# Fewer and smaller weight conversions in the last twelve ticks of attention

## The chip, the cores and the metric

The kernel runs on one NeuronCore of a Trainium2 chip. The metric is the time on the device in microseconds (us). Three runs of the kernel before took 709.95, 710.32 and 710.77 us; their median, 710.32 us, is the time before. The core's engines are TensorE (PE, with its weight loads as PEld), VectorE (DVE), ScalarE (ACT), GpSimd (POOL) and SyncE (SP), which only issues DMAs here. Each engine works through its own instructions in the order in which they are written, and waits on semaphores for the others.

## The reference, cut to what matters

Three stages, each feeding the next, all in float32:

- attention, for 2 batches of 8 heads, 768 positions, head size 64: scores `q k^T / 8`, masked where two hash buckets (signs of a projection to 6 values) differ, softmax over the row, times `v`;
- a dense layer on the 1536 rows of 512 values that come out: `h = x @ w_in` (512 to 2048), `g = s * max(h, 0)^2 + b`, `x2 = g @ w_out` (2048 to 512);
- a layer of 8 experts (512 to 1024 to 512) with one expert for each row, scaled by a softmax gate and a sigmoid gate.

## The kernel before, in words

**Attention** is a loop of 96 ticks (`tick`). A tick handles 128 query rows of one head against 768 keys. A pair of heads takes 12 ticks, and three ticks with one head's half of the queries form a trio. In tick t TensorE computes the scores `sp` (L264, L265); VectorE takes the row maximum `nm` (L267) and adds a constant to the sum of the tick before (`rd`, L272), then takes its reciprocal (L316); ScalarE computes the exponentials `pe` with their row sum (L323); GpSimd scales `pe` of the tick before by the reciprocal (L317). Three ticks later TensorE turns the probabilities around in two groups of three blocks (`tp`, L284) and each group is copied out of PSUM into `pt` (L312). At the end of each trio TensorE multiplies three of those blocks for both heads with `v` (`xp`, L333). `sp` has two buffers, so the scores of tick t+2 wait for the exponentials of tick t; `tp` has two buffers too, so the transposes of a tick wait for the copies of the tick before.

Within a tick, ScalarE's queue holds the copies of `tp` first and the exponentials behind them. VectorE's queue holds `nm`, `rd`, in some ticks the second copy of `tp`, the reciprocal, the low halves of attention's output (`xl`, L319), and last a piece of a weight conversion where there is one. The second copy is VectorE's in ticks whose number modulo 12 is 3, 4 or 6 (`VCOPY`), and in the drain (ticks 96 and later). In ticks 0 to 83 the queues also hold the preparation of the next pair of heads; ticks 84 to 95 belong to the last pair and have none. The ticks named below are 84 to 95.

**Dense-layer weights** come from HBM as 16 blocks of 1 MB, each holding a column block of `w_in` and a row block of `w_out` (k = 0 and 1). `stage(j)` loads block j as two tiles `stg` (512 KB each; five buffers; blocks 10 and 13 use a tile `tmp` instead). `conv(j)` turns each into a high part and a low part in the format that the matmuls want: per k, VectorE does L358, L360 and L364 into `cvm`, ScalarE rounds the result to the high part (L365), and VectorE subtracts to get the low part (L367). `conv` is a generator; what stands between two `yield`s is issued in one go. In the kernel before it has three pieces: both L358 and both L360; both L364, both L365 and the first L367; the second L367. In ticks 84 to 95 one piece follows each tick: blocks 0, 1 and 2 take ticks 84 to 92, and ticks 93 to 95 have none.

**The dense layer** (`moe1`) runs 48 steps, 16 for each third of the rows. Step s issues two ticks of attention's drain while there are any, then the 12 matmuls of `mm1` with block s mod 16 (L380), the nonlinearity of step s-1 (`elem` on ScalarE, `elem2` on VectorE, whose L402 writes `gl`), and the 12 matmuls of `mm2` for step s-2 (L418 to L420). Steps 0 to 12 stage block s+5 and convert block s+3 in one go. In VectorE's queue the conversion stands ahead of `gl` of step s-1; in ScalarE's, behind `elem`. A step is 24 matmuls.

Of the kernel before, what the change touches and what calls it, by code (L numbers as in the profile page):

```python
# [14 lines left out]
ALU = mybir.AluOpType  # L15
# [26 lines left out]
VCOPY = (3, 4, 6)  # L42
# [3 lines left out]
class Kernel:  # L46
# [190 lines left out]
    def tick(self, t):  # L237
        nc = self.nc
        NQ = 96
# [20 lines left out]
        if t < NQ:  # L260
            sp = self.ps2.tile([128, 2, 512], F32, tag="big", name="sp")
            for m in range(2):
                k = slice(m * HS, (m + 1) * HS)
# [11 lines left out]
        if 0 <= a < NQ:  # L275
            pe3, _ = st["pe"].pop(a)
# [10 lines left out]
        if t >= 15 and (t - 15) % 6 == 0:  # L287
# [11 lines left out]
            while lo < t0 + HS:  # L299
                g, c = divmod(lo, GW)  # L300
# [8 lines left out]
                lo = hi  # L309
        run("act")  # L310
        for j, c in enumerate(tps):
            (nc.vector.tensor_copy if j and (t % 12 in VCOPY or t >= NQ) else nc.scalar.copy)(*c)  # L312
        run("pool")
        run("dve")
        if 1 <= t < NQ + 1:
# [32 lines left out]
            nc.sync.dma_start(out=t, in_=self.ins["wio"][j, k])  # L348
            self.stg[j, k] = t

    def conv(self, j):
        nc = self.nc
        pool = self.wpool(j)
        self.w[j] = pool.tile([128, 2, 2, 512], F32R, tag="w", name="w")
        t = [self.stg.pop((j, k)) for k in range(2)]
        m = [self.cv_p.tile([128, 512], I32, name="cvm", bufs=4) for k in range(2)]
        for k in range(2):
            nc.vector.tensor_scalar(m[k], t[k][:, :, 1], 3, 0x3FFFFFFF, ALU.logical_shift_left, ALU.bitwise_and)  # L358
        for k in range(2):
            nc.vector.scalar_tensor_tensor(m[k], t[k][:, :, 1], -0x40000000, m[k], ALU.bitwise_and, ALU.bitwise_or)  # L360
        yield
        w = self.w[j]
        for k in range(2):
            nc.vector.scalar_tensor_tensor(m[k], t[k][:, :, 0], 29, m[k], ALU.logical_shift_right, ALU.bitwise_or)  # L364
            nc.scalar.copy(w[:, k, 0, :], m[k].bitcast(F32))  # L365
        for k in range(2):
            nc.vector.tensor_tensor(w[:, k, 1, :], m[k].bitcast(F32), w[:, k, 0, :].bitcast(F32), ALU.subtract)  # L367
            yield
# [566 lines left out]
    def moe1(self, ticks):  # L935
        self.h, self.g, self.y = {}, {}, {}
        gates = iter(())
        seq = self.sequence(0, NSTAT, {2})
        sp = iter(())
        self.ring, self.nring, self.nht, self.lq, self.regs, self.routed = {}, 0, 0, [], {}, False  # L940
        self.xg, self.xt, self.ht, self.hs, self.yps, self.hts = {}, {}, {}, {}, {}, []
        ns = 16 * NG
        for s in range(ns + 2):
            g, j = divmod(s, 16)
            for _ in range(2):
                next(ticks, None)
            c = s + 3
            cv = iter(())
            if c < 16:
                if c + 2 < 16:  # L950
                    self.stage(c + 2)
                cv = self.conv(c)
            if s < ns:
                self.mm1(s)
            if s > ns - 15:
                next(gates, None)
            if 1 <= s < ns + 1:
                self.elem(s - 1)
            for _ in cv:
                pass  # L960
            if 1 <= s < ns + 1:
                self.elem2(s - 1)
            if s >= 2:
                self.mm2(s - 2, gates if s > ns - 15 else iter(()))
                if (s - 2) % 16 == 15:
                    for _ in gates:
                        pass
                    gates = self.gate((s - 2) // 16)
                    if s == ns - 15:
                        self.x_es.close()  # L970
                        self.m2_p = self.m2_open()
                        gates = chain(gates, self.route_early())
            next(gates, None)
            for k in range(AHEAD):
                if s == ns + (-4, -3, -1, 0)[k]:
                    sp = chain(sp, self.split(seq[k], True))
            for _ in range(3):
                next(sp, None)
            if s == ns - 2:
                self.tx(0)  # L980
        for _ in sp:
            pass
        self.moe2(seq, chain(gates, self.route()), NSTAT)
# [28 lines left out]
    def build(self):  # L1012
        tc = self.tc
        with ExitStack() as es:
            ent = es.enter_context
            sb = lambda n, b, side="left": tc.tile_pool(name=n, bufs=b, side=side, reuse_waits="tile")
            ps = lambda n, b: tc.tile_pool(name=n, bufs=b, space=PSUM, reuse_waits="tile")
            dr = ent(tc.tile_pool(name="dr", bufs=1, space=DRAM))
            self.x2d = dr.tile([TOK, XW], F32, name="x2d")
            ent(tc.manual_schedule())  # L1020
            cst = ent(sb("cst", 1))
            self.stg_p = ent(sb("stg", 5))
            self.sg_p = ent(sb("sg", 1))
            self.ps1 = ent(ps("ps1", 1))
            ps_es = ExitStack()
            self.ps2 = ps_es.enter_context(ps("ps2", 2))
            self.x_es = ExitStack()
            self.x3_p = ent(sb("x3", 1, "right"))
            self.x_p = self.x_es.enter_context(sb("x", 1, "right"))
            self.m2_open = lambda: ent(sb("m2", 1, "right"))  # L1030
            self.stg, self.w = {}, {}
            self.consts(cst)
            e1 = ExitStack()
            r1 = lambda n, b: e1.enter_context(sb(n, b, "right"))
            self.v_p, self.xs_p, self.sm_p = r1("v", 3), r1("xs", 1), r1("sm", 6)
            self.p_p, self.pt_p = r1("pp", 5), r1("ptp", 4)
            e2 = ExitStack()
            r2 = lambda n, b: e2.enter_context(sb(n, b, "right"))
            self.qk_p, self.bit_p = r2("qk", 2), r2("bit", 2)
            self.cv_p = ent(sb("cv", 1))  # L1040
            with sb("d", 2, "right") as self.d_p:
                self.attention()
            self.w_p = [ent(sb("wa", 3))]

            def convs():
                for c in range(3):
                    for _ in self.conv(c):
                        yield
                    self.stage(c + 2)
            cv = convs()  # L1050
            for t in range(84, 96):
                self.tick(t)
                next(cv, None)
            for _ in cv:
                pass
            e2.close()
            ps_es.close()
            self.ps4 = ent(ps("ps4", 4))
            self.w_p.append(ent(sb("wb", 5)))
            self.g_p = ent(sb("g", 2))  # L1060

            def drain():
                for t in range(96, 107):
                    self.tick(t)
                    if t == 106:
                        e1.close()
                        self.w_p.append(ent(sb("wc", 8)))
                    yield
            self.moe1(drain())
            if "x2" in self.debug:  # L1070
                self.nc.sync.dma_start(out=self.debug["x2"], in_=self.x2d)
            self.T = self.nc.values_load(self.ev[0:1, 40:41], min_val=0, max_val=NMAX - 2)  # L1072
            self.extra(NSTAT)
# [67 lines left out]
```

## Time and profile before

| | |
|---|---|
| median of three runs | 710.32 us |
| profiled execution | 710.86 us |
| its span, first to last instruction | 709.1 us |
| PE busy | 679.8 us (96%) |
| DVE busy | 486.0 us (69%) |
| ACT busy | 421.9 us (60%) |
| POOL busy | 166.9 us (24%) |
| mean granted TensorE clock | 0.993 of full |

All positions in time are microseconds from the start of the profiled execution's span. Busy time of an engine is the time that its instructions cover. A line of a timeline gives start, duration, engine, source line, operation, tiles and shape; "x2" merges two neighbours, whose second starts before the first's end is recorded, so a pair's duration is less than twice that of one. In square brackets stands how long the engine was idle ahead of it, and who ended that.

### The profile page before, as it was taken

Reading aid. Unit: us, or ns where it says so; the run is one execution under the profiler, and the core shown is the slowest. Engines: PE = TensorE matmul, PEld = TensorE weight load, DVE = VectorE, ACT = ScalarE, POOL = GpSimd, SP = SyncE. Lnnn points to the kernel's source line nnn. Section 1 sums busy time; section 2 is a strip of 40 time slices with the busy share of each in tenths; the row PEclk is TensorE's granted clock in tenths of the full one; section 3 lists DMA queues with packets and bytes.
Section 4 is the critical chain, followed back from the end, with each engine's and each line's share of the span. In section 5 each row is a group of like instructions: output and inputs, shape, how many; then the busy total and the mean of one; then the engine's idle time right before and its main releaser. Section 6 shows DMA issues by size and latency. Waiting matters only on the chain. (4 is left out here: it accounts for less than half of the span.)

```text
span 709.1 us, 10423 instructions
## 1 busy us (share of the span) xinstructions
PE 679.8 (96%) x3696; PEld 512.4 (72%) x3696; DVE 486.0 (69%) x945; ACT 421.9 (60%) x756; POOL 166.9 (24%) x182
## 2 busy tenths in 40 slices
PE   6799999999997899999999999999999899999995
PEld 3566666666765567888877888788888688888863
DVE  4977778868779888993333432463357998998980
ACT  3778778878785756665212222222344688888870
POOL 4655555655554410000000000001000121212111
PEclk9999999999999999999999999999999999999999
DMA  9943261450601336520000020028301262101482
GB/s 205 242 93 95 62 157 37 120 140 19 215 1 61 119 119 238 196 72 1 0 1 1 0 61 0 1 61 357 147 1 48 58 223 90 59 31 56 151 298 110
DMA packets 17577, 69.89 MB, mean 99 GB/s; under 512 B 2990, under 2 KB 3886, under 8 KB 14064
## 3 DMA queue, kind: packets, MB, share of 16 engines
q1 hardware_dynamic: 15472, 62.61, 28.5%
q0 software_dynamic: 2048, 6.56, 2.7%
q8 instruction: 31, 0.51, 0.3%
q14 instruction: 26, 0.21, 0.1%
HBM read 100.61 MB, written 6.43 MB: 151 GB/s over the span
## 5 line engine op out<-in xcount | busy, mean ns | idle before, releaser
L380 PE MATMUL h<-xh,w 128*128 128x512 f32 x384 | 129.9, 399 | 0.0
L773 DVE TENSOR_TENSOR ring<-raw,ring 128x1024 fp32r<-128x1024 f32 x96 | 113.6, 1222 | 11.5 <-ACT ring L771 10.4
L267 DVE TENSOR_REDUCE nm<-sp 128x1 f32<-128x768 f32 x96 | 91.3, 951 | 39.2 <-PE sp L265 38.4
L317 POOL TENSOR_SCALAR pe<-pe,rd 128x768 f32<-128x768 f32 x96 | 91.1, 949 | 108.0 <-DVE rd L316 47.4
L323 ACT ACTIVATE pe<-sp,nm 128x768 f32<-128x768 f32 x96 | 87.4, 910 | 20.5 <-DVE rd L272 16.0
L771 ACT CAST ring<-raw 128x1024 fp32r<-128x1024 f32 x96 | 96.4, 1054 | 1.6 <-DMA raw<-w 1.6
L312 ACT COPY pt<-tp 128x384 f32<-128x384 f32 x165 | 72.3, 487 | 28.1 <-PE tp L284 27.8
L284 PE MATMUL tp<-consts,pe 128*128 128x128 f32 x576 | 80.8, 277 | 5.8 <-POOL pe L317 2.3
L380 PEld LDWEIGHTS h<-xh,w 128*128 128x128 f32 x384 | 72.2, 188 | 18.4 <-issue 2.0
L264 PE MATMUL sp<-ka,qa 128*128 128x384 f32 x192 | 75.6, 394 | 7.1 <-ACT pe L323 5.1
L284 PEld LDWEIGHTS tp<-consts,pe 128*128 128x128 f32 x576 | 67.4, 142 | 15.6 <-POOL pe L317 8.6
L380 PE MATMUL h<-xl,w 128*128 128x512 f32 x192 | 76.0, 396 | 0.0
L396 ACT ACTIVATE gh<-r,sb 128x512 fp32r<-128x512 f32 x34 | 24.7, 725 | 85.5 <-PE y L420 42.8
L418 PE MATMUL y<-w,gh 128*128 128x512 f32 x192 | 75.5, 393 | 0.0
L419 PE MATMUL y<-w,gl 128*128 128x512 f32 x192 | 75.0, 391 | 0.0
L420 PE MATMUL y<-w,gh 128*128 128x512 f32 x192 | 74.9, 390 | 0.0
L333 PE MATMUL xp<-pt,v 128*64 128x384 f32 x384 | 70.2, 502 | 0.1
L265 PE MATMUL sp<-kb,qb 128*128 128x384 f32 x192 | 65.7, 342 | 0.0
L387 ACT ACTIVATE r<-h 128x512 f32<-128x512 f32 x48 | 28.8, 599 | 60.8 <-PE h L380 35.1
L264 PEld LDWEIGHTS sp<-ka,qa 128*128 128x128 f32 x192 | 36.9, 192 | 35.8 <-ACT pe L323 20.5
L404 DVE SCALAR_TENSOR_TENSOR gl<-r,sb,gh 128x512 fp32r<-128x512 f32 x34 | 25.6, 752 | 51.7 <-ACT gh L396 51.7
L625 POOL DMA_INDIRECT xg<-x2d,ix x2 | 2.3, 1145 | 213.9 <-DVE r L395 213.6
(234 smaller groups left out, 1156.7 us busy)
## 6 DMA issues: line engine op xcount, KB each, us to landing
raw<-w SPq DMA_DIRECT2D x56, 1024.0 KB
stg<-wio SPq DMA_DIRECT2D x28, 512.0 KB
d<-qk SPq DMA_DIRECT2D x14, 768.0 KB
dz<-qz SPq DMA_DIRECT2D x14, 384.0 KB
x2d<-x SPq DMA_DIRECT2D x12, 256.5 KB
v<-v SPq DMA_DIRECT2D x8, 384.0 KB
tmp<-wio SPq DMA_DIRECT2D x4, 512.0 KB
d<-qk SPq DMA_DIRECT2D x4, 384.0 KB
```

Of the source, the lines that this page charges most:

```text
L264: nc.tensor.matmul(sp[:, m, 0:HS], QA[h][:, q], KA[h][:, k], start=True, stop=False)
L267: nc.vector.tensor_reduce(nm, sp[:, :, 0:HS], AX.XY, ALU.max, negate=True)
L284: nc.tensor.transpose(tp[:, kt, :], pe3[:, (3 * j + kt) * 128:(3 * j + kt + 1) * 128], self.ident)
L312: (nc.vector.tensor_copy if j and (t % 12 in VCOPY or t >= NQ) else nc.scalar.copy)(*c)
L317: nc.gpsimd.tensor_scalar(pe, pe, rd, 1.0, ALU.mult, ALU.mult)
L323: nc.scalar.activation(pe.rearrange("p (n k) -> p n k", n=2), sp[:, :, 0:HS], AF.Exp, bias=nm, accum_out=den)
L380: nc.tensor.matmul(h, a, b, start=(n == 0), stop=(n == 11))
L418: nc.tensor.matmul(y, gh[:, c], w[:, 0], start=(j == 0), stop=False)
L419: nc.tensor.matmul(y, gl[:, c], w[:, 0], start=False, stop=False)
L420: nc.tensor.matmul(y, gh[:, c], w[:, 1], start=False, stop=(j == 15))
L771: nc.scalar.copy(t[:, 0], src)
L773: nc.vector.tensor_tensor(t[:, 1], src, t[:, 0].bitcast(F32), ALU.subtract)
```

## The change

Three edits. In ticks 84 to 95 the second copy of `tp` is ScalarE's as well, in all ticks (it was VectorE's in ticks 87, 88 and 90). The blocks converted in ticks 84 to 95 are 0 and 1 instead of 0, 1 and 2, with `conv` cut into six pieces: L358 and L360 of k = 0; the same of k = 1; L364 and L365 of k = 0; the same of k = 1; the two L367 apart. The twelve pieces fill the twelve ticks. In `moe1`, step s converts block s+2 instead of s+3 and stages block s+4 instead of s+5, in steps 0 to 13 instead of 0 to 12, and in one go as before.

```diff
-            (nc.vector.tensor_copy if j and (t % 12 in VCOPY or t >= NQ) else nc.scalar.copy)(*c)
+            (nc.vector.tensor_copy if j and (t % 12 in VCOPY and t < 84 or t >= NQ) else nc.scalar.copy)(*c)
...
-    def conv(self, j):
+    def conv(self, j, fine=False):
...
         for k in range(2):
             nc.vector.tensor_scalar(m[k], t[k][:, :, 1], 3, 0x3FFFFFFF, ALU.logical_shift_left, ALU.bitwise_and)
-        for k in range(2):
-            nc.vector.scalar_tensor_tensor(m[k], t[k][:, :, 1], -0x40000000, m[k], ALU.bitwise_and, ALU.bitwise_or)
-        yield
+            if fine:
+                nc.vector.scalar_tensor_tensor(m[k], t[k][:, :, 1], -0x40000000, m[k], ALU.bitwise_and, ALU.bitwise_or)
+                yield
+        if not fine:
+            for k in range(2):
+                nc.vector.scalar_tensor_tensor(m[k], t[k][:, :, 1], -0x40000000, m[k], ALU.bitwise_and, ALU.bitwise_or)
+            yield
         w = self.w[j]
         for k in range(2):
             nc.vector.scalar_tensor_tensor(m[k], t[k][:, :, 0], 29, m[k], ALU.logical_shift_right, ALU.bitwise_or)
             nc.scalar.copy(w[:, k, 0, :], m[k].bitcast(F32))
+            if fine:
+                yield
         for k in range(2):
             nc.vector.tensor_tensor(w[:, k, 1, :], m[k].bitcast(F32), w[:, k, 0, :].bitcast(F32), ALU.subtract)
             yield
...
-            c = s + 3
+            c = s + 2
...
-                for c in range(3):
-                    for _ in self.conv(c):
+                for c in range(2):
+                    for _ in self.conv(c, True):
                         yield
                     self.stage(c + 2)
```

VectorE's queue from the reciprocal of tick 84 on, in the kernel before (`nm` opens the next tick; `cvm` is the conversion's work tile, `stg` the staged weights):

```order
L316 RECIPROCAL rd<-rd 128x1
L358 TENSOR_SCALAR cvm<-stg 128x512 x2
L360 SCALAR_TENSOR_TENSOR cvm<-stg,cvm 128x512 x2
L267 TENSOR_REDUCE nm<-sp 128x1
L272 TENSOR_SCALAR rd<-den 128x1
L316 RECIPROCAL rd<-rd 128x1
L364 SCALAR_TENSOR_TENSOR cvm<-stg,cvm 128x512 x2
L367 TENSOR_TENSOR w<-cvm,w 128x512
```

The same queue from the same instruction on, with the change (L368 is the old L364):

```order
L316 RECIPROCAL rd<-rd 128x1
L358 TENSOR_SCALAR cvm<-stg 128x512
L360 SCALAR_TENSOR_TENSOR cvm<-stg,cvm 128x512
L267 TENSOR_REDUCE nm<-sp 128x1
L272 TENSOR_SCALAR rd<-den 128x1
L316 RECIPROCAL rd<-rd 128x1
L358 TENSOR_SCALAR cvm<-stg 128x512
L360 SCALAR_TENSOR_TENSOR cvm<-stg,cvm 128x512
L267 TENSOR_REDUCE nm<-sp 128x1
L272 TENSOR_SCALAR rd<-den 128x1
L316 RECIPROCAL rd<-rd 128x1
L368 SCALAR_TENSOR_TENSOR cvm<-stg,cvm 128x512
```

Between two `nm` there now stand two conversion instructions or one, where there were four or three, and the first piece now comes twice for a block, in two ticks running.

ScalarE's queue from the exponentials of tick 85 on, in the kernel before (`xs` is a copy of attention's output `xp` that falls into tick 87):

```order
L323 ACTIVATE pe,den<-sp,nm 128x768
L365 CAST w<-cvm 128x512 x2
L312 COPY pt<-tp 128x3x128 x2
L323 ACTIVATE pe,den<-sp,nm 128x768
L294 COPY xs<-xp 128x384
L312 COPY pt<-tp 128x3x128
L323 ACTIVATE pe,den<-sp,nm 128x768
L312 COPY pt<-tp 128x3x128
```

The same queue with the change, from the exponentials of tick 86 on (L369 is the old L365):

```order
L323 ACTIVATE pe,den<-sp,nm 128x768
L369 CAST w<-cvm 128x512
L294 COPY xs<-xp 128x384
L312 COPY pt<-tp 128x3x128 x2
L323 ACTIVATE pe,den<-sp,nm 128x768
L369 CAST w<-cvm 128x512
L312 COPY pt<-tp 128x3x128 x2
L323 ACTIVATE pe,den<-sp,nm 128x768
```

Ticks 86 and 87 now each end in one L369, and ticks 87 and 88 have both copies on ScalarE. TensorE's, SP's and GpSimd's instructions keep their order.

## Rows read from the trace of the kernel before

**Rows 1.** Windows: ticks 72 to 83, then the four trios of ticks 84 to 95.
```profile
core 0: us, PE busy (x) PEld busy (x) DVE busy (x) ACT busy (x) POOL busy (x), PEclk, DMA share, GB/s
184.65:212.90 28.25, 28.01 (x183) 19.48 (x181) 22.14 (x53) 22.73 (x52) 15.65 (x19) 1.00 0.19 71
212.90:219.69 6.79, 6.62 (x45) 4.80 (x43) 5.71 (x12) 3.59 (x9) 1.98 (x3) 1.00 0.00 0
219.69:232.48 12.79, 9.10 (x45) 5.15 (x43) 12.46 (x26) 7.81 (x18) 4.95 (x6) 0.87 0.33 119
232.48:239.56 7.08, 6.92 (x44) 4.72 (x43) 6.73 (x15) 4.20 (x10) 3.04 (x3) 1.00 0.23 85
239.56:248.77 9.21, 7.16 (x43) 4.69 (x43) 7.16 (x17) 8.04 (x19) 5.48 (x6) 1.00 0.32 114
```

**Rows 2.** Waits, 212.90 to 248.77: us in total, times, longest.
```profile
ACT pe L323 <- DVE rd L272: 8.8, 7, 2.6
PE sp L264 <- ACT pe L323: 3.0, 5, 1.2
PE tp L284 <- DVE pt L312: 2.0, 1, 2.0
```

**Rows 3.** Timeline of PE: scores of ticks 85 to 87; `xp` after ticks 86 and 89.
```profile
214.29 0.42 PE L264 MATMUL sp<-ka,qa 128*128 128x384 f32 x1
216.05 0.44 PE L264 MATMUL sp<-ka,qa 128*128 128x384 f32 x1 [0.17 <-ACT pe L323]
...
217.60 2.16 PE L333 MATMUL xp<-pt,v 128*64 128x384 f32 x12
219.69 0.44 PE L264 MATMUL sp<-ka,qa 128*128 128x384 f32 x1
...
229.14 3.41 PE L333 MATMUL xp<-pt,v 128*64 128x384 f32 x12
```

**Rows 4.** Timeline of DVE: tick 84 up to the piece of tick 85.
```profile
213.91 0.96 DVE L267 TENSOR_REDUCE nm<-sp 128x1 f32<-128x768 f32 x1 [2.03 <-PE sp L265]
...
215.05 0.75 DVE L358 TENSOR_SCALAR cvm<-stg 128x512 int32<-128x512 int32 x2
215.71 1.94 DVE L360 SCALAR_TENSOR_TENSOR cvm<-stg,cvm 128x512 int32<-128x512 int32 x2
217.56 0.95 DVE L267 TENSOR_REDUCE nm<-sp 128x1 f32<-128x768 f32 x1
...
218.68 1.27 DVE L364 SCALAR_TENSOR_TENSOR cvm<-stg,cvm 128x512 int32<-128x512 int32 x2
```

**Rows 5.** Timeline of ACT: exponentials, casts and copies of ticks 85 and 86.
```profile
218.60 0.90 ACT L323 ACTIVATE pe<-sp,nm 128x768 f32<-128x768 f32 x1 [1.86 <-DVE rd L272]
...
219.49 1.13 ACT L365 CAST w<-cvm 128x512 fp32r<-128x512 f32 x2
220.52 0.86 ACT L312 COPY pt<-tp 128x384 f32<-128x384 f32 x2
```

**Rows 6.** Timeline of POOL: scaling without, and with, a conversion beside it.
```profile
212.07 0.91 POOL L317 TENSOR_SCALAR pe<-pe,rd 128x768 f32<-128x768 f32 x1 [0.67 <-DVE rd L316]
215.32 1.17 POOL L317 TENSOR_SCALAR pe<-pe,rd 128x768 f32<-128x768 f32 x1 [2.35 <-PE sp L265]
```

**Rows 7.** Windows: around the slow `xp`; dense steps 0 to 12; the steps behind them.
```profile
228.30:232.50 4.20, 4.19 (x16) 1.67 (x16) 4.08 (x10) 2.58 (x7) 1.02 (x1) 0.59 0.33 110
250.60:322.00 71.40, 71.40 (x322) 54.77 (x321) 64.97 (x119) 47.69 (x78) 3.32 (x4) 1.00 0.43 155
322.00:341.40 19.40, 19.40 (x86) 15.83 (x85) 5.07 (x8) 7.29 (x12) 0.00 (x0) 1.00 0.00 1
```

**Rows 8.** Timelines of DVE, end of the conversion of step 0, and PE, start of step 2.
```profile
254.60 1.29 DVE L367 TENSOR_TENSOR w<-cvm,w 128x512 fp32r<-128x512 f32 x2
...
261.40 0.50 PE L380 MATMUL h<-xh,w 128*128 128x512 f32 x1
```

**Rows 9.** Waits of SP, 200 to 330.
```profile
SPq L348 <- DVE cvm L364: 105.2, 22, 31.3
```

## The prediction

> **What bounds the kernel now.** I read the table of windows first, cut at the trios of the last twelve ticks, then the waits of that stretch, then the timelines of the engines named there.
>
> The windows [rows 1] give the place. Ticks 72 to 83, which prepare a pair of heads beside their own work, take 28.25 us with PE busy for 28.01. Ticks 84 to 95 have less to do on PE and take 6.79 + 12.79 + 7.08 + 9.21 = 35.87 us. The reader is to see that the first trio is PE's own pace: 6.79 us, of which 0.17 is a wait [rows 3], so 6.62 us. Four such trios are 26.5 us, and 9.4 us are lost: 0.2, 6.2, 0.5 and 2.6. In the worst trio DVE is busy for 12.46 of 12.79 us and PE for 9.10. So DVE is the bound there.
>
> The waits [rows 2] show how that reaches PE: exponentials wait for DVE seven times, 8.8 us in all; scores wait for the exponentials, 3.0 us; and once the transposes wait 2.0 us for a copy in DVE's queue. Behind that wait PE's granted clock falls: 0.59 in 228.30 to 232.50 [rows 7], a mixture of 2.4 and 1.2 GHz. The `xp` in it takes 3.41 us [rows 3]; the one after tick 86 took 2.16. So 1.2 us of the loss is the slow clock.
>
> Behind the stretch PE is busy without a gap: 71.40 of 71.40 us in steps 0 to 12, 19.40 of 19.40 in those behind [rows 7]. What is won ahead of that stretch should arrive at the end, as long as nothing there becomes late.
>
> **What comes off DVE.** Block 2's conversion: a first piece of 2.51 us (215.05 to 217.56 [rows 4]), two L364 (1.27), and two L367, which I price like L364, 0.64 each. That is 5.1 us. The three copies I price like those on ACT, 0.43 each (0.86 for two [rows 5]), 1.3 together. DVE was busy for 5.71 + 12.46 + 6.73 + 7.16 = 32.1 us [rows 1]; about 25.7 stay, below PE's 26.5. So the sum no longer binds, and what is left depends on the order within a tick.
>
> **The first piece, where I had to choose.** Alone, one L358 and one L360 should take 0.33 (half of 215.05 to 215.71) plus 0.64 (half of the L364 pair, the same operation), so 1.0 us. But two L360 took 1.94 where two L364 took 1.27 [rows 4]: 0.67 more. Beside them GpSimd's scaling starts at 215.32 and takes 1.17 instead of 0.91 [rows 6]; it ends at 216.49, and L360 ends 1.16 later, about two free L360. I read that as L360 standing still until GpSimd was done. In a small piece L358 starts 0.27 ahead of the scaling, and L360 needs L358's result, so GpSimd comes in between the two again: L360 starts about 216.3 and the piece takes 1.85 us. If L360 slips in ahead it takes 1.0. The bounds are 1.0 and 2.5 (as long as the whole old piece); I take 1.85, the case nearest to the row. The pieces of one instruction start 0.28 us ahead of the scaling, as the L364 pair did at its full speed, and count 0.64.
>
> The Trainium skill has a rule on this that speaks against small pieces ("SBUF — State Buffer", section "Who interferes with whom"): VectorE and GpSimd share a pair of ports that one instruction holds to its end, VectorE's instructions with two SBUF inputs want it, and whoever issues first keeps the other out. The 1.94 against 1.27 us agrees with it. By the rule each of the four small first pieces loses once, as in my choice; without it the sum would be that of the first rival below, 702.9.
>
> **Trio by trio.** Constants: `nm` to the piece 1.14 us and `nm` to the scores two ticks on 2.14 (213.91 to 215.05 and to 216.05) [rows 3, 4]; `nm` to exponentials 1.04 (217.56 to 218.60), exponentials 0.89 (to 219.49), one cast 0.57, two copies 0.8, `xs`, a copy of the same size, 0.4 [rows 4, 5]; one tick of PE 1.39 (212.90 to 214.29).
> First trio: unchanged to `nm` at 213.91. Then `nm` of tick 85 at 215.05 + 1.85 = 216.90, of 86 at 219.89, of 87 at 219.89 + 1.14 + 0.64 = 221.67. PE starts tick 87 at 219.69 as now. So 6.8 us.
> Second trio: scores of tick 88 cannot start before 219.89 + 2.14 = 222.03; PE would be there at 219.69 + 1.39 = 221.08, so it waits 0.95. ACT: exponentials of 86 from 220.93 to 221.82, cast to 222.4, `xs` to 222.8, two copies to 223.6, exponentials of 87 to 224.5. So the scores of tick 89 start at 224.6, where PE would be at 223.4: 1.2 more. One more cast and two copies end at 225.9, on which the transposes of tick 89 wait some 0.2. Loss 2.2 to 2.3, the trio 8.8 us. Here the moved copies and the casts cost something: ACT runs without a pause in that trio.
> By tick 90 PE is at 228.5 and both others have caught up, so the second half repeats the first: 6.9 and 8.8 us. No wait is as long as the 2.0 us ahead of the slow clock. In the fourth trio now, which loses 2.6 us in waits, the clock is 1.00 [rows 1], so I count full speed.
> Sum: 6.8 + 8.8 + 6.9 + 8.8 = 31.3 against 35.87: 4.6 us less.
>
> **The shift in the dense layer.** Each step's conversion stays where it was in DVE's queue, with the next lower block. Block 2 is now done when step 0's slot ends, 254.60 + 1.29 = 255.9, and step 2 wants it at 261.40 [rows 8]: 5.5 us of cover, so nothing; without that cover the delay would fall on PE one for one. The fourteenth slot, in step 13, meets a DVE that is busy for 5.07 of 19.40 us [rows 7]; at 4.6 us a slot it fits, and only `gl` of step 12 stands behind it, wanted by `mm2` most of a step later. ACT's two casts there (1.13 us) meet 7.29 of 19.40. The stagings go through SP in the same order. All of SP's waits there, 22 times, are for L364 to free a buffer [rows 9], so each load follows the conversion that frees it, and the next use is two slots on, as now. The loads of blocks 2 and 3 have several ticks.
>
> The profiled execution took 710.86 us, so 706.3 by its own clock. It lies 0.5 above the median of the runs; on the median 710.32 - 4.6 = 705.7 us.
>
> **The rivals.**
> *L360 is not held up (more gain).* `nm` of 85 comes at 216.05 and of 86 at 218.2; tick 88 does not wait; ACT's queue in the second trio still has `xs`, two casts and six copies and costs about 0.8 a half. The stretch is 26.5 + 0.4 + 1.6 = 28.5 us, 7.4 less: 702.9. For it: ticks 72 to 83 take 28.25 with DVE busy for 22.14 and ACT for 22.73 [rows 1]. Against it: the 1.94.
> *The clock falls in both halves.* Each fall costs 1.2 us of `xp`: 4.6 - 2.4 = 2.2 gained, 708.1. For it: two waits of about 1 us follow each other within 3 us. Against it: the fourth trio now.
> *Nothing changes.* PE's waits would have another cause, GpSimd's scaling say, and the stretch would stay at 35.9: 710.3. Against it: the rows of waits name DVE and its dependants.
> *Weights come late (slower).* Block s+2 instead of s+3 leaves one slot less between conversion and `mm1`. If a staged block came so late that DVE's slots stood 5.5 us further behind PE, `mm1` would wait, and DVE, busy for 64.97 of 71.40 us [rows 7], could hardly catch up. From 5.5 + 4.6 = 10.1 us of lateness on the kernel would be slower; at 13 us, 713.2. For it: every load hangs on a buffer. Against it: the slots would have to slip by two steps, and the distance from release to use stays.
>
> **Chances.** The forecast, 0.50; L360 free or otherwise more gain, 0.26; clock falls, 0.11; nothing changes, 0.07; weights late, 0.06. I call a change within 0.2% (1.4 us) no change, about what a measurement can tell here. The first three are faster: 0.87; same 0.07; slower 0.06. The likeliest case alone spans gains of 3.5 to 6. The range runs from the better rival with a little more (8.1) to the clock rival, 702.2 to 708.2; outside lie the last two rivals and a little at the ends.
>
> **What would show it.** Windows of the four trios near 6.8, 8.8, 6.9, 8.8 us at clock 1.00; single L360 in ticks 84, 85, 90, 91 at about 1.3 us against 0.68; no PE wait ahead of L380 in steps 2 to 15; PE without a gap behind 250. It is wrong if the trios with casts lose much more than 2.3 us, if PE waits for a block of weights, or if the time won in the ticks is missing at the end.

## The result, and the profile after

| | before | with the change |
|---|---|---|
| median | 710.55 us (4 runs) | 704.71 us (4 runs, 704.16 to 705.35) |
| ratio | | 0.9913 (95% interval 0.9900 to 0.9926) |
| profiled execution | 710.86 us | 705.0 us |
| its span | 709.1 us | 703.2 us |

The change makes the kernel 5.8 us faster; 4.6 were predicted, and 704.71 lies in the range.

The windows of the changed kernel over ticks 72 to 83 and the four trios, as in [rows 1] (window, its length, busy time and number of instructions of PE, PEld, DVE, ACT, POOL, granted clock, DMA share, GB/s):

```profile
185.17:213.42 28.25, 28.02 (x182) 19.46 (x180) 22.15 (x53) 22.73 (x52) 15.75 (x19) 1.00 0.17 66
213.42:220.20 6.78, 6.63 (x44) 4.80 (x42) 5.64 (x11) 4.25 (x10) 1.91 (x3) 1.00 0.00 0
220.20:228.44 8.24, 7.26 (x44) 4.66 (x42) 7.84 (x18) 7.23 (x16) 4.55 (x6) 1.00 0.41 129
228.44:235.22 6.78, 6.63 (x44) 4.80 (x42) 5.64 (x11) 4.46 (x12) 2.57 (x3) 1.00 0.00 1
235.22:243.46 8.24, 7.26 (x44) 4.68 (x42) 7.19 (x18) 7.34 (x17) 5.62 (x5) 1.00 0.38 128
```

6.78, 8.24, 6.78 and 8.24 us stand where [rows 1] had 6.79, 12.79, 7.08 and 9.21: 30.04 us instead of 35.87. Both halves are now alike, and the clock is full throughout. The difference, 5.83 us, is as large as the whole result (710.55 - 704.71 = 5.84). The waits of the same stretch (who waited for whom, us in total, times, longest) answer to [rows 2]:

```profile
ACT pe L323 <- DVE rd L272: 4.2, 5, 1.0
PE sp L264 <- ACT pe L323: 1.4, 6, 0.3
PE tp L284 <- ACT pt L312: 0.8, 2, 0.4
```

Exponentials wait 4.2 us for DVE instead of 8.8, scores 1.4 us for them instead of 3.0, and the 2.0 us wait for DVE's copy is gone. What is left begins with the first pieces. DVE's timeline in ticks 84 and 85, then the piece of tick 86 (start, duration, instruction), answers to [rows 4]:

```profile
214.43 0.96 DVE L267 TENSOR_REDUCE nm<-sp 128x1 f32<-128x768 f32 x1 [2.02 <-PE sp L265]
...
215.56 0.41 DVE L358 TENSOR_SCALAR cvm<-stg 128x512 int32<-128x512 int32 x1
216.00 1.28 DVE L360 SCALAR_TENSOR_TENSOR cvm<-stg,cvm 128x512 int32<-128x512 int32 x1
217.21 0.94 DVE L267 TENSOR_REDUCE nm<-sp 128x1 f32<-128x768 f32 x1
...
221.10 0.67 DVE L368 SCALAR_TENSOR_TENSOR cvm<-stg,cvm 128x512 int32<-128x512 int32 x1
```

GpSimd's scaling beside that first piece answers to [rows 6]:

```profile
215.84 0.91 POOL L317 TENSOR_SCALAR pe<-pe,rd 128x768 f32<-128x768 f32 x1 [2.33 <-PE sp L265]
```

The one L360 takes 1.28 us, while L368, an operation of the same kind and size, takes 0.67. The scaling that starts while L358 still runs, 0.16 us ahead of L360, takes its free 0.91 us: this time DVE alone pays. The piece is 1.65 us long (215.56 to 217.21).

How that reaches PE in the second trio is seen in ACT's timeline, tick 86 to 87:

```profile
221.01 0.90 ACT L323 ACTIVATE pe<-sp,nm 128x768 f32<-128x768 f32 x1 [1.02 <-DVE rd L272]
...
221.91 0.61 ACT L369 CAST w<-cvm 128x512 fp32r<-128x512 f32 x1
222.41 0.48 ACT L294 COPY xs<-xp 128x384 f32<-128x384 f32 x1
222.78 0.87 ACT L312 COPY pt<-tp 128x384 f32<-128x384 f32 x2
223.53 0.93 ACT L323 ACTIVATE pe<-sp,nm 128x768 f32<-128x768 f32 x1
```

and in PE's, ticks 88 and 89:

```profile
222.06 0.44 PE L264 MATMUL sp<-ka,qa 128*128 128x384 f32 x1 [0.23 <-ACT pe L323]
...
223.42 0.85 PE L284 MATMUL tp<-consts,pe 128*128 128x128 f32 x6 [0.40 <-ACT pt L312]
224.60 0.44 PE L264 MATMUL sp<-ka,qa 128*128 128x384 f32 x1 [0.34 <-ACT pe L323]
```

The exponentials of tick 86 are late by DVE; behind them ACT runs cast, `xs`, copies and exponentials without a pause, and PE waits for each. (The idle time in brackets is shorter than what the wait costs, since a matmul's recorded end overlaps the next one's start.)

Behind the stretch, the windows of dense steps 0 to 12 and of those behind them, as in [rows 7]:

```profile
245.30:316.70 71.40, 71.40 (x322) 54.76 (x321) 64.98 (x119) 47.70 (x78) 3.33 (x4) 1.00 0.47 170
316.70:336.10 19.40, 19.40 (x86) 15.83 (x85) 9.34 (x16) 8.32 (x14) 0.00 (x0) 1.00 0.00 1
```

PE is as gapless as before. The fourteenth conversion is there (DVE 9.34 us instead of 5.07) and costs nothing. The end of step 0's conversion on DVE, now block 2, and the start of step 2 on PE, which wants it, answer to [rows 8]:

```profile
249.30 1.29 DVE L373 TENSOR_TENSOR w<-cvm,w 128x512 fp32r<-128x512 f32 x2
```
```profile
256.10 0.50 PE L386 MATMUL h<-xh,w 128*128 128x512 f32 x1
```

250.59 against 256.10: 5.5 us of cover, as before. One thing differs ahead of the stretch. The profile's row of the granted clock in 40 slices, before and with the change:

```profile
PEclk9999999999999999999999999999999999999999
```
```profile
PEclk7799999999999999999999999999999999999999
```

In this execution the clock was lower at the start, and tick 84 begins 0.5 us later (213.42 against 212.90). Nothing ahead of tick 84 was changed: in the kernels run here the `xp` behind tick 83 starts anywhere from 210.43 to 211.53. The dense layer therefore starts 5.3 us earlier than before. That stays 5.3 us until shortly before the end, where one group of 32 matmuls (L820, now L826) takes 4.05 us instead of 4.54. That group took 3.64 to 4.54 us in these kernels, so nothing ties the difference to the change. The two shifts of 0.5 us cancel by chance.

### The profile page after: what moved, and what is told of

The parts are those of the page before. It is cut to its first block, busy times and chain, and to the rows that moved or that the text cites. A ratio compares the mean times of both kernels' runs of the same rounds, so it can differ in the third digit from the quotient of the medians.

```text
span 703.2 us, 10422 instructions
## 1 busy us (share of the span) xinstructions
PE 678.5 (96%) x3696; PEld 513.1 (73%) x3696; DVE 484.2 (69%) x942; ACT 422.4 (60%) x759; POOL 166.2 (24%) x182
## 5 line engine op out<-in xcount | busy, mean ns | idle before, releaser
L317 POOL TENSOR_SCALAR pe<-pe,rd 128x768 f32<-128x768 f32 x96 | 89.2, 929 | 102.6 <-DVE rd L316 43.6
```

The lines of the kernel that those rows point to most:

```text
L317: nc.gpsimd.tensor_scalar(pe, pe, rd, 1.0, ALU.mult, ALU.mult)
```

## The experiments

For each kernel the table gives the stretch from the `xp` behind tick 83 to the `xp` behind tick 95, cut at the `xp` between, all from PE's timeline of its one profiled execution; the window starts 2.1 us earlier than that of [rows 1] and shares lost time a little differently among the trios. Times are medians, ratios go against the kernel before run beside them. e2 and e8 differ by 1.0 us in the stretch and not in the median, which lies within the intervals of the ratios; so the stretch, where instruction follows instruction, is the finer measure, though each is one execution.

| kernel | trios (us) | stretch | time (us) | ratio, 95% interval |
|---|---|---|---|---|
| before | 6.79, 11.54, 8.11, 9.43 | 35.87 | 710.3 to 710.6 | |
| e1: copies alone | 6.78, 10.08, 8.45, 9.19 | 34.50 | 709.35 | 0.9984 (0.9973 to 0.9995) |
| e8: third block away alone | 6.78, 11.17, 8.37, 6.80 | 33.12 | 707.83 | 0.9963 (0.9949 to 0.9977) |
| e2: third block away, copies | 6.78, 9.36, 9.20, 6.78 | 32.12 | 707.96 | 0.9964 (0.9950 to 0.9978) |
| e3: third block away, small pieces | 6.78, 7.85, 6.74, 8.61 | 29.98 | 704.37 | 0.9913 (0.9897 to 0.9930) |
| the change, all three | 6.78, 8.24, 6.78, 8.24 | 30.04 | 704.71 | 0.9913 (0.9900 to 0.9926) |
| e5: one block in the ticks | 6.78, 8.24, 6.79, 6.78 | 28.59 | 703.97 | 0.9914 (0.9894 to 0.9935) |
| e4: first pieces cut otherwise | 6.79, 6.97, 6.78, 6.99 | 27.53 | 702.38 | 0.9886 (0.9870 to 0.9903) |
| e6: scaling left out in four ticks | 6.79, 7.05, 6.78, 7.06 | 27.68 | 795.54 | 1.1201 (1.1166 to 1.1236) |

**e1: the copies alone.** Against the kernel before:

```diff
-            (nc.vector.tensor_copy if j and (t % 12 in VCOPY or t >= NQ) else nc.scalar.copy)(*c)
+            (nc.vector.tensor_copy if j and (t % 12 in VCOPY and t < 84 or t >= NQ) else nc.scalar.copy)(*c)
```

> The kernel before with only the copies moved: in ticks 84 to 95 ScalarE makes both copies; three blocks in the old pieces. Theory queue (what is ahead of a late row maximum in VectorE's queue sets the pace): about 0.5 us come back for each of the copies of ticks 87 and 88, and the slow clock (1.2 us) should go with the 2.0 us wait of the transposes: stretch of the four trios 35.9 to about 33.5, 1.5 to 2.7 us faster than before, 708 to 709. Rival copy (the wait of the transposes for VectorE's copy, with the slow clock behind it, was most of the loss): 3.5 us or more, 707 or less.

Measured: 709.35 us, stretch 34.50. The rival falls: the wait for DVE's copy was not most of the loss. Theory queue had the sign, and its 33.5 missed by 1.0, its 708 to 709 by 0.35. The slow clock did not go with the 2.0 us wait; the windows of the second and third trio:

```profile
217.90:227.98 10.08, 8.40 (x43) 6.25 (x43) 9.76 (x22) 6.87 (x16) 5.26 (x5) 0.83 0.28 106
227.98:236.43 8.45, 7.09 (x43) 4.75 (x43) 8.29 (x18) 6.31 (x14) 3.34 (x3) 1.00 0.38 126
```

0.83 is again a time of 1.2 GHz, by estimate (1 - 0.83) x 2 x 10.08 = 3.4 us of it. PE's waits ahead of it were 0.47 and 1.21 us:

```profile
221.43 0.85 PE L284 MATMUL tp<-consts,pe 128*128 128x128 f32 x6 [0.47 <-ACT pt L312]
223.48 0.54 PE L264 MATMUL sp<-ka,qa 128*128 128x384 f32 x1 [1.21 <-ACT pe L323]
```

**e2: the change without the small pieces.** Against the change:

```diff
-                    for _ in self.conv(c, True):
+                    for _ in self.conv(c):
```

> The change without the small pieces: two blocks, converted in the old three pieces in ticks 84 to 89, copies on ScalarE. Theory queue: the first half stays bad (first trio 6.8, second about 11), the second half has no conversion (6.8 and 6.9): stretch about 31.5, 0.8 to 1.8 us slower than the change, 705.5 to 706.5. Rival amount (only the third block counted, the size of the pieces does not): the same as the change, 704.7.

Measured: 707.96 us, stretch 32.12; slower than the change by 2.1 us in the stretch, more than the 0.8 to 1.8 expected. The rival falls: the size of the pieces counts. My miss lies in the second block, whose old pieces in ticks 87 to 89 hold up the third trio as well, which I had put at 6.8; the second, put at about 11, took less. Second and third trio:

```profile
217.88:227.24 9.36, 7.32 (x43) 4.60 (x42) 9.08 (x19) 6.55 (x15) 5.28 (x5) 1.00 0.31 112
227.24:236.44 9.20, 7.07 (x43) 4.74 (x42) 8.31 (x19) 7.28 (x17) 3.95 (x4) 1.00 0.32 118
```

**e3: the change without the moved copies.** Against the change:

```diff
-            (nc.vector.tensor_copy if j and (t % 12 in VCOPY and t < 84 or t >= NQ) else nc.scalar.copy)(*c)
+            (nc.vector.tensor_copy if j and (t % 12 in VCOPY or t >= NQ) else nc.scalar.copy)(*c)
```

> The change with the copies of ticks 87, 88 and 90 back on VectorE. Theory queue, by hand: in ticks 87 and 88 ScalarE is the late one, so it gains 0.3 to 0.8 us there; in tick 90 the copy stands ahead of a late maximum and costs about 0.4: within 0.6 us of the change, 704.2 to 705.2. Rival copy: the wait of the transposes for VectorE comes back, 2 us or more slower than the change, 706.7 or more.

Measured: 704.37 us, stretch 29.98. The second trio gains 0.4 us and the fourth loses 0.4, with the signs that the theory gave, and the sum is nothing. The rival falls. With small pieces the moved copies bring nothing; with the old pieces they bring 1.0 us (e8 against e2; the medians, 707.83 and 707.96, do not show it). The second and fourth trio:

```profile
218.20:226.05 7.85, 7.24 (x43) 4.70 (x42) 7.75 (x21) 6.70 (x16) 4.46 (x6) 1.00 0.32 106
232.79:241.40 8.61, 7.27 (x43) 4.67 (x42) 8.20 (x19) 7.08 (x16) 5.07 (x5) 1.00 0.37 118
```

**e8: the third block away, nothing else.** The edits of e2 and e3 together; against the kernel before that is:

```diff
-            c = s + 3
+            c = s + 2
...
-                for c in range(3):
+                for c in range(2):
```

> The kernel before with block 2's conversion moved out of the ticks (two blocks, later step), old pieces, copies of ticks 87, 88 and 90 on VectorE. Theory queue, from the traces so far: first and second trio as before (6.8 and 11.5, slow clock included), third about 8, fourth 6.8 since nothing is converted from tick 90 on: stretch about 33, 2.3 to 3.0 us faster than before, 707.3 to 708. So moving the block out would be under half of the change's 5.8. Rival amount (the third block is nearly all of the gain): 705.5 or less.

Measured: 707.83 us, stretch 33.12, as expected. So moving block 2 out of the ticks gives by itself 2.75 of the 5.83 us. PE's timeline in the second trio has the old picture, wait and slow `xp`:

```profile
229.00 0.55 PE L284 MATMUL tp<-consts,pe 128*128 128x128 f32 x3 [1.98 <-DVE pt L312]
229.48 3.30 PE L333 MATMUL xp<-pt,v 128*64 128x384 f32 x12
```

**e4: the first two pieces cut otherwise.** Against the change; the instructions are the same:

```diff
         for k in range(2):
             nc.vector.tensor_scalar(m[k], t[k][:, :, 1], 3, 0x3FFFFFFF, ALU.logical_shift_left, ALU.bitwise_and)
-            if fine:
-                nc.vector.scalar_tensor_tensor(m[k], t[k][:, :, 1], -0x40000000, m[k], ALU.bitwise_and, ALU.bitwise_or)
-                yield
-        if not fine:
-            for k in range(2):
-                nc.vector.scalar_tensor_tensor(m[k], t[k][:, :, 1], -0x40000000, m[k], ALU.bitwise_and, ALU.bitwise_or)
+        if fine:
             yield
+        for k in range(2):
+            nc.vector.scalar_tensor_tensor(m[k], t[k][:, :, 1], -0x40000000, m[k], ALU.bitwise_and, ALU.bitwise_or)
+        yield
```

> The change with the first two pieces cut otherwise: both L358 in tick 84 (and 90), both L360 in tick 85 (and 91); the same instructions. Theory port (L360 at 1.28 us stands still beside GpSimd's scaling, which slips in because L360 waits for L358): an L360 that starts ahead of the scaling takes 0.68, the pair 1.3; the row maximum of tick 86 comes 1.4 us earlier; second and fourth trio 8.24 to about 7.1 us each, stretch 30.0 to about 27.8, 702.5. Rival amount (the instructions cost what they cost, wherever they stand): the same as the change, 704.7.

Measured: 702.38 us, stretch 27.53, both within 0.3 us of what was expected. DVE's timeline, the pair in tick 85 (L362 is L360 here), and GpSimd's scaling beside it:

```profile
216.45 1.27 DVE L362 SCALAR_TENSOR_TENSOR cvm<-stg,cvm 128x512 int32<-128x512 int32 x2
```
```profile
216.72 1.69 POOL L317 TENSOR_SCALAR pe<-pe,rd 128x768 f32<-128x768 f32 x1 [0.63 <-PE sp L265]
```

Two of them take 1.27 us, as long as one took in the change, and now the scaling waits (1.69 instead of 0.91), where nothing depends on it soon. Second and fourth trio shrink to 6.97 and 6.99:

```profile
217.22:224.19 6.97, 6.82 (x43) 4.72 (x43) 6.00 (x15) 6.33 (x16) 4.96 (x6) 1.00 0.37 120
230.97:237.96 6.99, 6.82 (x43) 4.73 (x42) 6.00 (x14) 6.36 (x16) 4.81 (x5) 1.00 0.38 128
```

It beats both kernels; 27.53 us is near PE's 26.5.

**e5: one block in the ticks.** Against the change:

```diff
-            c = s + 2
+            c = s + 1
...
-                for c in range(2):
+                for c in range(1):
```

> The change carried one block further: only block 0 is converted in the ticks (small pieces, ticks 84 to 89), step s converts block s+1. Theory cover: the stretch loses the fourth trio's 1.45 us (30.0 to 28.6); a step's first low part is ready about 1 us ahead of the matmuls that want it, so PE waits 0.3 us or less in all: 703.0 to 703.6. Rival late weights (one step of lead is not enough): waits of PE ahead of the dense matmuls in each of the first steps, 1.5 us or more in all, 704.5 or more.

Measured: 703.97 us (the profiled execution 703.07), stretch 28.59 against the 28.6 expected. The median lies 0.4 us above the 703.0 to 703.6 expected, and its ratio, 0.9914, is not distinct from the change's 0.9913: the 1.45 us show in the stretch alone. PE does not wait for weights, not even with a step less of lead. The window of steps 0 to 14, and the end of block 1's conversion on DVE with the start of step 1 on PE:

```profile
243.64:325.00 81.36, 81.36 (x365) 62.89 (x363) 74.47 (x136) 54.40 (x89) 3.30 (x4) 1.00 0.45 162
```
```profile
247.63 1.29 DVE L373 TENSOR_TENSOR w<-cvm,w 128x512 fp32r<-128x512 f32 x2
```
```profile
249.37 0.50 PE L386 MATMUL h<-xh,w 128*128 128x512 f32 x1
```

The pair ends at 248.92, 0.45 us before step 1 begins. The rival falls.

**e6: GpSimd's scaling left out in ticks 84, 85, 90 and 91.** The probabilities that these ticks would scale stay unscaled. Against the change:

```diff
-            nc.gpsimd.tensor_scalar(pe, pe, rd, 1.0, ALU.mult, ALU.mult)
+            if t not in (84, 85, 90, 91):
+                nc.gpsimd.tensor_scalar(pe, pe, rd, 1.0, ALU.mult, ALU.mult)
```

> The change with GpSimd's scaling left out in ticks 84, 85, 90 and 91, so four ticks' probabilities stay unscaled; everything else is the same. Theory port: with no scaling beside it the single L360 takes 0.68 instead of 1.28 although it still waits for its L358, the piece 1.05 instead of 1.65, and the second and fourth trio come to 7.0 to 7.4: stretch about 28.0. Rival hand-over (the 1.28 is the wait of L360 for L358's result): L360 stays at 1.28 and the stretch at 30.0.

Measured: stretch 27.68, the kernel 795.54 us. Only the stretch is compared: with other values the expert layer converts 120 pieces of weights instead of 96, and takes longer. DVE's L360 (L361 here) in tick 84:

```profile
216.03 0.69 DVE L361 SCALAR_TENSOR_TENSOR cvm<-stg,cvm 128x512 int32<-128x512 int32 x1
```

It still comes behind its L358 and takes 0.69 us. So the 1.28 is the scaling beside it, not the hand-over from L358, and without the scaling the second and fourth trio become 1.2 us shorter:

```profile
218.15:225.20 7.05, 6.82 (x43) 4.74 (x42) 6.28 (x16) 6.61 (x16) 3.83 (x5) 1.00 0.37 128
231.98:239.04 7.06, 6.80 (x43) 4.73 (x42) 6.31 (x16) 6.64 (x16) 3.70 (x4) 1.00 0.36 116
```

## Why the prediction was right, point by point

- **DVE bounds the stretch, and nothing behind it gives the time back.** Right: 5.83 us less in the stretch, no PE wait in the dense steps. DVE is busy for 26.3 us of the stretch (5.64 + 7.84 + 5.64 + 7.19), where 25.7 were counted.
- **The first piece is held up by GpSimd.** Right in kind, shown by e4 and e6 from two sides: the order and the neighbour decide, not the instructions. The Trainium skill's rule ("SBUF — State Buffer", section "Who interferes with whom": whoever issues first keeps the other out) agrees with both: L360 behind the scaling takes 1.28 us, and the scaling behind the L360 pair of e4 takes 1.69. By the recorded spans neither is kept out for quite that long: L360 ends 0.53 us behind the scaling (217.28 against 216.75), less than the 0.67 that it takes free.
- **The mis-sized term is the loss of the second and fourth trio**, put at 2.2 us each and measured at 1.6 (8.24 against 6.62). Its three waits, 0.95, 1.2 and 0.2, also add up to 2.35, of which the 8.8 us hold 2.2. The first piece was 1.65 us, not 1.85: `nm` starts 0.46 us behind the scaling's recorded end (217.21 against 216.75), where a whole free L360, 0.64, had been put. The piece counts twice before tick 86: row maximum of 86 at 6.55 us behind the scores of 84 (219.97 - 213.42), not 6.99. The rest is mostly ACT: from the end of the exponentials of tick 86 to the start of those of 87 it took 1.62 us (221.91 to 223.53), not 1.77. Twice 8.80 - 8.24 is 1.1 us of the 1.3 by which the sum of the trios, 31.3, lay above the measured 30.04; the third trio, put at 6.9 and measured at 6.78, is most of the rest.
- **Clock.** Full throughout, as counted. The rival with a fall in each half did not come. The reason that I gave, no wait as long as 2.0 us, is refuted by e1, where the clock fell with no wait above 1.21 us; so this part came true without its reason, by luck.
- **Copies.** I counted 1.3 us off DVE for them as part of the sum (on DVE they took 0.54 to 0.55 each, not 0.43). e3 shows that they add nothing in this change (29.98 against 30.04). By e8, e2 and the change, in that order, the gain is block 2 2.75, copies 1.00, small pieces 2.08; by e8, e3 and the change it is 2.75, pieces 3.14, copies -0.06. How much each edit is worth depends on what stands beside it.
- **Lead and loads.** Hidden, as said; e5 shows that one step less would be hidden too.

What a fall of the clock costs, 1.2 us in the prediction, was put too high. The second and third trio of e1 and of e2 hold the same instructions (block 2's first piece, in e1 alone, comes behind the last row maximum on which these trios wait). With the fall they took 10.08 + 8.45 = 18.53 us, without it 9.36 + 9.20 = 18.56. In the kernel before, DVE waited only 0.31 us for the scores behind the slow `xp`:

```profile
233.48 0.96 DVE L267 TENSOR_REDUCE nm<-sp 128x1 f32<-128x768 f32 x1 [0.31 <-PE sp L265]
```

By these rows most of the 1.2 us was time that PE would otherwise have spent waiting for DVE.

What stays open: why the clock fell in e1, with waits of 0.47 and 1.21 us ahead of it, and not in e2, where the same two waits (0.49, 1.21) were followed by 0.34, 1.28 and 0.76 us.

## What to carry to other kernels

Where an engine works through its queue in order, look at what stands ahead of the instruction on which others wait. The sum over a stretch does not give the loss: here the conversions of the same two blocks cost 2.1 us more in large pieces than in small ones (e2 against the change). When work for VectorE is cut into pieces beside GpSimd, see who issues first at each seam: here a dependent instruction that let GpSimd in between cost 2.5 us of the stretch, more than the moved copies brought in any of these kernels (1.4 at most). Before keeping a lead of several steps for data prepared beside a bound engine, measure the cover, since the earlier place may be the costlier one (here by 2.75 us of the stretch, e8).

## What the runs showed of the hardware

One such VectorE instruction (SCALAR_TENSOR_TENSOR, two operands in SBUF, 512 elements a partition) took 0.67 to 0.70 us in the change and in e6 when it started ahead of GpSimd's scaling or without it, and 1.28 us when the scaling had just started; the scaling took 0.91 us when it was first, and 1.69 us when two such instructions were. So one of the two paid 0.6 to 0.8 us, somewhat less than what was left of the other when it started (0.75 and 1.00 us by the recorded spans), and 0.16 and 0.27 us of order decided which one.
